# One ring of four PSUM banks in place of a bank for the keys and a ring of three

## The chip, the core and the metric

The kernel runs on one core of a Trainium2 chip. The metric is the device time of one execution in microseconds (us). The core's engines work from separate queues, each in its own order: TensorE (PE, with PEld for its weight loads), VectorE (DVE), ScalarE (ACT), GpSimd (POOL) and SyncE (SP), whose queue issues nearly all transfers here. Matmuls write to PSUM, which has eight banks, and ACT and DVE carry the results from there to SBUF.

## What is computed

Linear attention with a positive feature map, for 8 batches of 8 heads of 576 tokens, and then a mixer block on its output: mixing over the tokens, then over the channels.

```python
def phi(x):
    proj = np.einsum('bhsd,df->bhsf', x, w_phi)
    proj = proj - np.max(np.abs(proj), axis=-1, keepdims=True)
    return np.concatenate([np.exp(proj), np.exp(-proj)], axis=-1)
q_p, k_p = (phi(q), phi(k))
kv = np.einsum('bhsf,bhsd->bhfd', k_p, v)
z = np.sum(k_p, axis=2)
num = np.einsum('bhsf,bhfd->bhsd', q_p, kv)
den = np.einsum('bhsf,bhf->bhs', q_p, z)[..., None] + 1e-06
attention = num / den            # heads side by side become x: 8 x 576 x 512
xt = x.transpose(0, 2, 1)
h = np.maximum(xt @ w_tok1, 0.0) @ w_tok2
u = x + h.transpose(0, 2, 1)
h2 = np.maximum(u @ w_ch1, 0.0) @ w_ch2
out = u + h2
```

## The kernel before

Five streams are written as generators, and `weave` (L676) interleaves them in the program by the cost that each yields and a share given to it (L695). `keys()` (L283) goes over the 32 pairs of heads: it loads a pair (`raw`, `v`), splits it into a high and a low part (`stack`, tiles `stk`), projects five groups of tokens (`less_max`, L221, tiles `ppk`), and adds their exponentials `kp` into `pkv` (`add_kv`). `queries()` does the same for queries (`stq`, `ppq`, and the tail `ppt`), turns them, takes exponentials (`qf`, `qh`, `ql`) and multiplies them by the keys' sums (`numerators`, L504, tiles `pn`); the first eight pairs go another way (`pt`, `pr`, `pf`). `token_stream()` runs `token_mix` (L541) for each batch b in two halves h: transposes (`px`), a first product into `pa`, its relu (`ah` on ACT, `al` on DVE), and a second product into `ph`, which DVE adds to `xt` (L586). `channel_stream()` runs `channel_mix` (L590) on 18 blocks of 256 tokens, up (`h`, 24 matmuls for each of six tiles) and down (`acc`); a block starts when the batch it lies in is mixed. `load_weights()` brings in the weights. In a name such as `ph6_1_0_0` the first two numbers are the batch and the half; in `ppk30_1` and `pn28_01` the first is the pair of heads.

What is written so is not yet the order of the engines: from it a list scheduler makes each engine's queue, places the tiles, and adds the waits. It gives a tile a place when one of its pool is free, so that the number of banks in a pool decides which matmuls may come next.

The eight banks of PSUM: `ps_a` has two (`acc`, and the first batch's token mixing), `ps_h` one (`h`), `ps_k` one (`pkv`), and `ps_w` four. Three of these four form a ring, `REST` (L59), for queries, their turns, numerators, and token mixing from the second batch on (`bank`, L536). The fourth carries the tag "keys": the keys' projections (L236), every other projection of the first four pairs' queries (L233), and every other `h` of the last three blocks (L608). The keys' projections of the first four pairs are in `ps_a` (L227).

Of the kernel before, what the change touches and what calls it, by code (L numbers as in the profile page):

```python
# [8 lines left out]
F32 = mybir.dt.float32  # L9
# [8 lines left out]
P = 128  # L18
B, H, S, D = 8, 8, 576, 64
NP = H // 2  # L20
F = 128
# [16 lines left out]
CH = 256  # L38
# [9 lines left out]
def mixer_kernel(ctx, tc, qk, vm, vt, w_phi, w1, w2, wc1, wc2d, out):  # L48
# [5 lines left out]
    ps_w = ctx.enter_context(tc.tile_pool(name="ps_w", bufs=1, space=PSUM))  # L54
# [1 line left out]
    ps_h = ctx.enter_context(tc.tile_pool(name="ps_h", bufs=1, space=PSUM))  # L56
    ps_a = ctx.enter_context(tc.tile_pool(name="ps_a", bufs=1, space=PSUM))

    REST = dict(tag="rest", bufs=3)  # L59

    def streamed(pool, shape, dtype, **kw):

# [158 lines left out]
    def less_max(ts, units, name, base=None, early=False):  # L221

        n, kind = len(units), name[0]
        if early and base == D:
            ps = ps_a.tile([P, 2, 2, F], F32, tag=f"a{nplain['k'] % 2}", name=f"pp{name}")  # L227
            nplain["k"] += 1
        elif early and base == 0 and (nplain["q"] % 2 == 0 or nplain["q"] >= BORROWED):
            ps = ps_h.tile([P, 2, 2, F], F32, tag="h", name=f"pp{name}")  # L230
            nplain["q"] += 1
        elif early and base == 0:
            ps = ps_w.tile([P, 2, 2, F], F32, tag="keys", name=f"pp{name}", bufs=1)  # L233
            nplain["q"] += 1
        elif kind == "k":
            ps = ps_w.tile([P, 2, 2, F], F32, tag="keys", name=f"pp{name}", bufs=1)  # L236
        else:
            ps = ps_w.tile([P, 2, 2, F], F32, name=f"pp{name}", **REST)
        for i, u in enumerate(units):
            t, c = (ts[1], 512) if u is None else (ts[u[0]], P * u[1])  # L240
            if base is None:
                nc.tensor.matmul(ps[:, i].rearrange("p two f -> p (two f)"), t[:, c:c + P],  # L242
                                 wp2.rearrange("p two f -> p (two f)"), start=True, stop=True)
            else:
                rows = slice(D, P) if name == "k0_0" else slice(0, P)
                nc.tensor.matmul(ps[:, i, 0], t[rows, c:c + P], wz[rows, base // D], start=True, stop=True)  # L246
        if base is None:
            part = wk.tile([P, 2, F], F32, tag="part", name=f"part{name}")
            nc.scalar.copy(part[:, :n], ps[:, :n, 1])
            pr = wk.tile([P, 2, F], F32, tag="p", name=f"p{name}")  # L250
            nc.vector.tensor_tensor(pr[:, :n], ps[:, :n, 0], part[:, :n], op=ALU.add)
            pr, eng = pr[:, :n], nc.gpsimd
        else:
            pr, eng = ps[:, :n, 0], nc.vector
        mx = column(wk, 2, tag=f"mx{kind}", name=f"mx{name}")
        nc.vector.tensor_reduce(mx[:, :n], pr, axis=AX.X, op=ALU.max, apply_absolute_value=True)  # L256
        pm = wk.tile([P, 2, F], F32, tag=f"pm{kind}", name=f"pm{name}", bufs=1 if kind == "t" else 2)
        eng.tensor_tensor(pm[:, :n], pr, mx[:, :n].unsqueeze(2).to_broadcast([P, n, F]), op=ALU.subtract)  # L258
        return pm
# [160 lines left out]
    def turn(i, k, j, pm, tail, behind):  # L420
# [3 lines left out]
        else:  # L424
            ptr = ps_w.tile([P, 3, P], F32, **REST, name=f"pt{i}_{k}{j}")
            rows = [pm[:, 0], pm[:, 1]]
# [31 lines left out]
    def row_numerators(i, k, j, qps):  # L458
# [6 lines left out]
        if j == 0:  # L465
            sums[0] = ps_w.tile([P, 2, 3, D + 1], F32, **REST, name=f"pr{i}_{k}")
        pn = sums[0]
# [24 lines left out]
    def flip(i, k):  # L492
        b, p = divmod(i, NP)
        make_xts(b)
        x = rows_of[b, p // 2][k][:, :, (p % 2) * P:(p % 2) * P + P]
        pf = ps_w.tile([P, SEG[0][1]], F32, **REST, name=f"pf{i}_{k}")[:, :SEG[k][1]]
        for u in range(3 - k):
# [92 lines left out]
    def channel_mix(i, segs):  # L590
        uh, ul = [], []
        for c in range(NC_):
            h = streamed(wk, [P, CH], F32R, tag=f"uh{c}", name=f"uh{i}_{c}", bufs=1)
            l = streamed(wk, [P, CH], F32R, tag=f"ul{c}", name=f"ul{i}_{c}", bufs=1)
            d = 0
            for b, t, o, n, s in segs:
                nc.scalar.copy(h[:, d:d + n], t[:, c, o:o + n])  # L597
                nc.gpsimd.tensor_tensor(l[:, d:d + n], t[:, c, o:o + n], h[:, d:d + n].bitcast(F32),  # L598
                                        op=ALU.subtract)
                d += n  # L600
            uh.append(h)
            ul.append(l)
        yield 0
        acc = [ps_a.tile([P, 2, CH], F32, tag=f"a{k}", name=f"acc{i}_{k}") for k in range(2)]

        def up_proj(ep):
            if i >= LAST and ep % 2:
                ph = ps_w.tile([P, 2, CH], F32, tag="keys", name=f"h{i}_{ep}", bufs=1)  # L608
            else:
                ph = ps_h.tile([P, 2, CH], F32, tag="h", name=f"h{i}_{ep}")  # L610
            for k in range(2):
                es = slice((2 * ep + k) * P, (2 * ep + k + 1) * P)
                for c in range(NC_):
                    mm3(ph[:, k], (wc1_h[:, c, es], wc1_l[:, c, es]), (uh[c], ul[c]), c == 0, c == NC_ - 1)
            gh = streamed(wk, [P, 2, CH], F32R, tag="g", name=f"gh{i}_{ep}", bufs=4)
            gl = streamed(wk, [P, 2, CH], F32R, tag="g", name=f"gl{i}_{ep}", bufs=4)
            nc.scalar.activation(gh, ph, AF.Relu)  # L617
            nc.vector.scalar_tensor_tensor(gl, ph, 0.0, gh.bitcast(F32), op0=ALU.max, op1=ALU.subtract)  # L618
            return gh, gl

        def down_proj(ep, gh, gl):
            for a in range(2):
                for k in range(2):
                    e = 2 * ep + k
                    for c in (2 * a, 2 * a + 1):
                        cs = slice(c * P, (c + 1) * P)
                        mm3(acc[a][:, c % 2], (wc2[e][:, 0, cs], wc2[e][:, 1, cs]), (gh[:, k], gl[:, k]),
                            e == 0 and c % 2 == 0, e == NE - 1, group_ok=True)

        prev = None  # L630
        for ep in range(NE // 2):
            yield from until(lambda: 2 * ep + 1 in loaded)
            g = up_proj(ep)
            ups[0] += 1
            yield 2.6
            if prev is not None:
                yield from until(lambda: 2 * ep - 1 in loaded)
                down_proj(ep - 1, *prev)
                yield 2.6
            prev = g  # L640
        yield from until(lambda: NE - 1 in loaded)
        down_proj(NE // 2 - 1, *prev)
        yield 2.6
        for k in range(2):
            d = 0
            for b, t, o, n, s in segs:
                v = t[:, 2 * k:2 * k + 2, o:o + n]
                nc.vector.tensor_tensor(v, acc[k][:, :, d:d + n], v, op=ALU.add)
                nc.sync.dma_start(out[b, :, 2 * k:2 * k + 2, s:s + n], v)
                d += n  # L650
        yield 0
# [87 lines left out]
```

## Time and profile before

| What | Value |
|---|---|
| median of three runs | 1119.68 us (1118.68 to 1120.17) |
| the profiled execution, its own time | 1120.8 us |
| span of its trace | 1119.0 us |
| granted TensorE clock, mean | 0.995 |
| PE busy, share of the span | 98% |
| weight loads (PEld) | 96% |
| DVE, ACT, POOL | 63%, 50%, 51% |

An engine's busy share is of the whole span. Matmuls overlap in the records (one of 256 columns has a row of some 280 ns), so that PE reads busy while its matmuls follow more slowly than they could; the number of matmuls in a stretch (the x in brackets) tells more than the busy time. A wait is put down to the instruction that released it.

### The profile page before, as it was taken

The page shows a single profiled execution, that of the slowest core. Times are in us where ns is not written, and L with a number is a line of the kernel's source. Part 1 is how long each engine was busy: PE and PEld are TensorE (multiplying, and loading weights), DVE is VectorE, ACT ScalarE, POOL GpSimd, SP SyncE. Part 2 cuts the span into 40 slices and gives each one's busy share as a digit, 9 for nine tenths or more (in the row PEclk, how much of TensorE's full clock was granted, in tenths as well). Part 3 has the DMA queues.
Part 4 walks back from the last instruction along what each step waited for, and adds up shares of the span by engine and source line. Part 5 has one row for each costly group of instructions (what it writes and reads, how often), then busy time and mean ns, then how long its engine had stood idle before and what let it go on. Part 6 is the DMA issues. An engine that isn't in the chain of part 4 may idle for free.

```text
span 1119.0 us, 24637 instructions
## 1 busy us (share of the span) xinstructions
PE 1092.4 (98%) x9040; PEld 1073.2 (96%) x9040; DVE 708.9 (63%) x1775; ACT 556.1 (50%) x1589; POOL 567.0 (51%) x1047
## 2 busy tenths in 40 slices
PE   9999999999999999999999999999999989999998
PEld 8998999989998899999999999999999989999998
DVE  6889964467667676767666575764776776642111
ACT  4766553345546464656545464454565656441110
POOL 2334342367647665766656484663675766430110
PEclk9999999999999999999999999999999999999999
DMA  8545401133313232333323232122332232200000
GB/s 204 170 135 151 133 28 52 34 94 78 87 30 92 74 76 71 85 84 75 74 60 80 57 95 69 53 66 70 76 75 63 75 85 45 62 21 20 20 20 19
DMA packets 186744, 82.73 MB, mean 74 GB/s; under 512 B 159424, under 2 KB 171200, under 8 KB 186624
## 3 DMA queue, kind: packets, MB, share of 16 engines
q1 hardware_dynamic: 185104, 80.74, 27.9%
q8 instruction: 71, 1.16, 0.4%
q10 hardware_dynamic: 1520, 0.43, 0.2%
q14 instruction: 49, 0.40, 0.1%
HBM read 57.54 MB, written 23.59 MB: 73 GB/s over the span
## 4 chain that ended last, share of the span: by engine, by line
PE 77%; DVE 9%; POOL 4%; DMA 3%; ACT 3%; issue 2%; SPq 1%; ACTq 0%; POOLq 0%; DVEq 0%
PE h L87 24%; PE acc L87 23%; PE pkv L327 8%; PE pn L87 6%; PE ph L87 4%; PE pa L87 4%; PE pr L472 2%; PE ppk L242 2%; PE ppq L242 2%; DMA raw<-in_qk 1%; PE px L551 1%; DMA v<-in_vm 1%; PE ppq L246 1%; POOL pmq L258 1%; DMA qt<-dq 1%
## 5 line engine op out<-in xcount | busy, mean ns | idle before, releaser
L87 PE MATMUL acc<-gh,wc 128*128 128x256 f32 x1728 | 337.6, 282 | 0.0
L87 PEld LDWEIGHTS acc<-gh,wc 128*128 128x128 f32 x1728 | 273.6, 188 | 0.2
L87 PE MATMUL h<-uh,wc_h 128*128 128x256 f32 x864 | 244.1, 283 | 3.5 <-DVE gl L618 3.1
L87 PE MATMUL h<-uh,wc_l 128*128 128x256 f32 x864 | 244.1, 283 | 0.0
L87 PE MATMUL h<-ul,wc_h 128*128 128x256 f32 x864 | 242.9, 281 | 0.8 <-POOL ul L598 0.8
L87 PE MATMUL acc<-gl,wc 128*128 128x256 f32 x864 | 239.8, 281 | 0.0
L87 PEld LDWEIGHTS h<-uh,wc_h 128*128 128x128 f32 x864 | 162.5, 188 | 5.5 <-PE pn L87 2.8
L87 PEld LDWEIGHTS h<-ul,wc_h 128*128 128x128 f32 x864 | 162.7, 188 | 1.2 <-POOL ul L598 1.0
L87 PEld LDWEIGHTS acc<-gl,wc 128*128 128x128 f32 x864 | 162.5, 188 | 0.0
L87 PEld LDWEIGHTS h<-uh,wc_l 128*128 128x128 f32 x864 | 162.5, 188 | 0.0
L327 PE MATMUL pkv<-v,kp 128*128 128x65 f32 (+2 forms) x1152 | 160.2, 270 | 1.8 <-ACT kp L302 0.7
L327 PEld LDWEIGHTS pkv<-v,kp 128*128 128x128 f32 x1152 | 150.5, 192 | 3.5 <-ACT kp L302 1.6
L302 ACT ACTIVATE kp<-pmk 128x256 f32<-128x256 f32 (+1 forms) x320 | 108.5, 389 | 67.1 <-POOL pmk L258 43.9
L618 DVE SCALAR_TENSOR_TENSOR gl<-h,gh 128x512 fp32r<-128x512 f32 x108 | 73.5, 680 | 98.2 <-ACT gh L617 95.0
L447 POOL TENSOR_TENSOR ql<-qf,qh 128x320 fp32r<-128x320 f32 (+1 forms) x96 | 80.1, 834 | 72.4 <-ACT qh L446 72.1
L617 ACT ACTIVATE gh<-h 128x512 fp32r<-128x512 f32 x108 | 64.4, 596 | 101.1 <-PE h L87 99.4
L438 ACT ACTIVATE qf<-qt 128x320 f32<-128x320 f32 (+1 forms) x192 | 81.6, 437 | 63.0 <-POOL qf L437 29.0
L87 PE MATMUL pn<-qh,kv 128*128 128x320 f32 (+1 forms) x384 | 106.6, 308 | 3.8 <-ACT qh L446 1.6
L598 POOL TENSOR_TENSOR ul<-xt,uh 128x64 fp32r<-128x64 f32 (+3 forms) x120 | 60.6, 530 | 92.3 <-ACT uh L597 92.3
L446 ACT ACTIVATE qh<-qt 128x320 fp32r<-128x320 f32 (+1 forms) x192 | 82.9, 436 | 29.1 <-POOL qh L445 27.0
L217 POOL TENSOR_TENSOR stk<-raw,stk 64x512 fp32r<-64x512 f32 (+1 forms) x48 | 68.3, 1422 | 47.7 <-DVE stk L216 45.2
L258 POOL TENSOR_TENSOR pmk<-pk,mxk 128x256 f32<-128x256 f32 (+1 forms) x120 | 72.8, 606 | 36.0 <-DVE mxk L256 27.8
(129 smaller groups left out, 2293.1 us busy)
## 6 DMA issues: line engine op xcount, KB each, us to landing
raw<-in_qk SPq DMA_DIRECT2D x23, 576.0 KB, 4.2
rawc<-in_wc SPq DMA_DIRECT2D x24, 512.0 KB, 4.1
v<-in_vm SPq DMA_DIRECT2D x31, 256.0 KB, 4.1
dq<-tq SPq DMA_DIRECT2D x24, 320.0 KB, 2.1
qt<-dq SPq DMA_DIRECT2D x96, 80.0 KB, 2.9
dq<-tq SPq DMA_DIRECT2D x24, 256.0 KB, 2.0
qt<-dq SPq DMA_DIRECT2D x96, 64.0 KB, 2.9
out_x<-xt SPq DMA_DIRECT2D x12, 256.0 KB, 2.1
```

Source lines behind the costliest of these rows:

```text
L87: nc.tensor.matmul(o, a, m, start=first and i == 0, stop=last and i == 2, skip_group_check=group_ok)
L217: nc.gpsimd.tensor_tensor(t[lo:lo + D], src, t[base:base + D].bitcast(F32), op=ALU.subtract)
L242: nc.tensor.matmul(ps[:, i].rearrange("p two f -> p (two f)"), t[:, c:c + P], wp2.rearrange("p two f -> p (two f)"), start=True, stop=True)
L258: eng.tensor_tensor(pm[:, :n], pr, mx[:, :n].unsqueeze(2).to_broadcast([P, n, F]), op=ALU.subtract)
L302: nc.scalar.activation(kp[:, :len(us), sg], pm[:, :len(us)], AF.Exp, scale=1.0 - 2.0 * sg)
L327: nc.tensor.matmul(o, kp[:, n, sg], v, start=g == 0 and n == 0 and sg == 0, stop=u is None, skip_group_check=True)
L438: nc.scalar.activation(full, src, AF.Exp, scale=1.0 - 2.0 * sg)
L446: nc.scalar.activation(hi, src, AF.Exp, scale=1.0 - 2.0 * sg)
L447: (nc.gpsimd if sg else nc.vector).tensor_tensor(lo, full, hi.bitcast(F32), op=ALU.subtract)
L598: nc.gpsimd.tensor_tensor(l[:, d:d + n], t[:, c, o:o + n], h[:, d:d + n].bitcast(F32), op=ALU.subtract)
L617: nc.scalar.activation(gh, ph, AF.Relu)
L618: nc.vector.scalar_tensor_tensor(gl, ph, 0.0, gh.bitcast(F32), op0=ALU.max, op1=ALU.subtract)
```

## The change

The ring `REST` gets four banks in place of three, and the three uses of the tag "keys" become uses of the ring. The keys' projections therefore take whichever of the four banks comes free, as do all the others, and the others may take the bank that was the keys'. The number of banks in all stays at eight. No instruction is added or taken away: both programs have 8152 matmul instructions, with the same count for every tile's name and shape.

```diff
--- before.py
+++ after.py
@@ -56,7 +56,7 @@
     ps_h = ctx.enter_context(tc.tile_pool(name="ps_h", bufs=1, space=PSUM))
     ps_a = ctx.enter_context(tc.tile_pool(name="ps_a", bufs=1, space=PSUM))
 
-    REST = dict(tag="rest", bufs=3)
+    REST = dict(tag="rest", bufs=4)
 
     def streamed(pool, shape, dtype, **kw):
 
@@ -230,10 +230,10 @@
             ps = ps_h.tile([P, 2, 2, F], F32, tag="h", name=f"pp{name}")
             nplain["q"] += 1
         elif early and base == 0:
-            ps = ps_w.tile([P, 2, 2, F], F32, tag="keys", name=f"pp{name}", bufs=1)
+            ps = ps_w.tile([P, 2, 2, F], F32, name=f"pp{name}", **REST)
             nplain["q"] += 1
         elif kind == "k":
-            ps = ps_w.tile([P, 2, 2, F], F32, tag="keys", name=f"pp{name}", bufs=1)
+            ps = ps_w.tile([P, 2, 2, F], F32, name=f"pp{name}", **REST)
         else:
             ps = ps_w.tile([P, 2, 2, F], F32, name=f"pp{name}", **REST)
         for i, u in enumerate(units):
@@ -605,7 +605,7 @@
 
         def up_proj(ep):
             if i >= LAST and ep % 2:
-                ph = ps_w.tile([P, 2, CH], F32, tag="keys", name=f"h{i}_{ep}", bufs=1)
+                ph = ps_w.tile([P, 2, CH], F32, name=f"h{i}_{ep}", **REST)
             else:
                 ph = ps_h.tile([P, 2, CH], F32, tag="h", name=f"h{i}_{ep}")
             for k in range(2):
```

What it moves is the order that the scheduler makes. Three places follow; the rows are the instructions of one engine in their order.

First, PE at token mixing of batch 6, second half: the end of the first product, `pa6_1`, and the start of the second, `ph6_1`. Before:

```order
L87 MATMUL pa6_1_13908<-xh6_1_4_14078,w1_l_103 128x256
L327 MATMUL pkv29_13822<-v1_113,kp29_4_14098 128x2x65
L242 MATMUL ppk30_1_14255<-wp2_91,stk300_14130 128x256 x2
L87 MATMUL ph6_1_0_0_14109<-w2_h_104,ah6_1_14105 128x320
L87 MATMUL ph6_1_0_0_14109<-w2_l_105,ah6_1_14105 128x320
L87 MATMUL ph6_1_1_0_14117<-w2_h_104,ah6_1_14105 128x320
L87 MATMUL ph6_1_1_0_14117<-w2_l_105,ah6_1_14105 128x320
L242 MATMUL ppt29_14156<-wp2_91,stq291_14153 128x256
```

Now:

```order
L87 MATMUL pa6_1_13908<-xh6_1_4_14078,w1_l_103 128x256
L87 MATMUL ph6_1_0_0_14109<-w2_h_104,ah6_1_14105 128x320
L87 MATMUL ph6_1_0_0_14109<-w2_l_105,ah6_1_14105 128x320
L87 MATMUL ph6_1_1_0_14117<-w2_h_104,ah6_1_14105 128x320
L242 MATMUL ppk30_0_14136<-wp2_91,stk300_14130 128x256 x2
L87 MATMUL ph6_1_1_0_14117<-w2_l_105,ah6_1_14105 128x320
L327 MATMUL pkv29_13822<-v1_113,kp29_4_14098 128x2x65 x2
L242 MATMUL ppt29_14156<-wp2_91,stq291_14153 128x256
```

The key group `ppk30_1` and one matmul of `pkv29` stood between the last `pa6_1` and the first `ph6_1`; now nothing does. The group `ppk30_0`, which stood earlier still, is now among the `ph6_1`, and `ppk30_1` comes some 40 rows below. `pn28_01`, which stands ten rows below both pieces, took the bank that `ph6_1_0_0` had left; in the built program it now takes the one of `ppt29`.

Second, DVE at the same place, with the semaphores that each instruction waits for in brackets (DMAHW is a transfer). Before:

```order
L577 SCALAR_TENSOR_TENSOR al6_1_14106<-pa6_1_13908,ah6_1_14105 128x512 [waits Activation_49]
L251 TENSOR_TENSOR pt29_14160<-ppt29_14156,partt29_14158 128x128 [waits Activation_49,Pool_49]
L216 CAST stk310_14607<-raw31_14602 64x512 [waits DMAHW6_49]
L586 TENSOR_TENSOR xt0_6_11788<-ph6_1_0_0_14109,xt0_6_11788 128x320 [waits PE_49]
L256 TENSOR_REDUCE mxt29_14162<-pt29_14160 128x1 [waits DVE_49]
L586 TENSOR_TENSOR xt0_6_11788<-ph6_1_1_0_14117,xt0_6_11788 128x320 [waits PE_49]
L251 TENSOR_TENSOR pq29_00_14171<-ppq29_00_14166,partq29_00_14169 128x256 [waits Activation_49,Pool_49]
```

Now:

```order
L577 SCALAR_TENSOR_TENSOR al6_1_14106<-pa6_1_13908,ah6_1_14105 128x512 [waits Activation_49]
L251 TENSOR_TENSOR pk30_0_14141<-ppk30_0_14136,partk30_0_14139 128x256 [waits Activation_49]
L256 TENSOR_REDUCE mxk30_0_14143<-pk30_0_14141 128x2 [waits DVE_49]
L251 TENSOR_TENSOR pt29_14160<-ppt29_14156,partt29_14158 128x128 [waits Activation_49,Pool_49]
L586 TENSOR_TENSOR xt0_6_11788<-ph6_1_0_0_14109,xt0_6_11788 128x320 [waits PE_49]
L256 TENSOR_REDUCE mxt29_14162<-pt29_14160 128x1 [waits DVE_49]
L586 TENSOR_TENSOR xt0_6_11788<-ph6_1_1_0_14117,xt0_6_11788 128x320 [waits PE_49]
L251 TENSOR_TENSOR pq29_00_14171<-ppq29_00_14166,partq29_00_14169 128x256 [waits Activation_49,Pool_49]
```

The cast `stk310`, which waits for a transfer, stood ahead of the two adds of `ph6_1` to `xt`; now it stands 14 rows behind the first of them. The two steps of `ppk30_0` have come in ahead of `pt29`.

Third, PE at token mixing of batch 3, first half. Before:

```order
L87 MATMUL pa3_0_6152<-xl3_0_4_6366,w1_h_102 128x256
L87 MATMUL pa3_0_6152<-xh3_0_4_6365,w1_l_103 128x256
L87 MATMUL h5_0_6462<-uh5_3_6454,wc1_l_107 128x256
L87 MATMUL ph3_0_0_0_6420<-w2_h_104,ah3_0_6416 128x320
L87 MATMUL ph3_0_0_0_6420<-w2_l_105,ah3_0_6416 128x320
L87 MATMUL ph3_0_1_0_6491<-w2_h_104,ah3_0_6416 128x320
L87 MATMUL ph3_0_1_0_6491<-w2_l_105,ah3_0_6416 128x320
```

Now:

```order
L87 MATMUL h5_0_6462<-uh5_1_6442,wc1_l_107 128x256
L87 MATMUL h5_0_6462<-uh5_2_6448,wc1_h_106 128x256
L87 MATMUL h5_0_6462<-ul5_2_6449,wc1_h_106 128x256
L87 MATMUL h5_0_6462<-uh5_2_6448,wc1_l_107 128x256
L87 MATMUL h5_0_6462<-uh5_3_6454,wc1_h_106 128x256
L87 MATMUL h5_0_6462<-ul5_3_6455,wc1_h_106 128x256
L87 MATMUL h5_0_6462<-uh5_3_6454,wc1_l_107 128x256
L87 MATMUL ph3_0_0_0_6420<-w2_h_104,ah3_0_6416 128x320
L87 MATMUL ph3_0_0_0_6420<-w2_l_105,ah3_0_6416 128x320
L87 MATMUL ph3_0_1_0_6491<-w2_h_104,ah3_0_6416 128x320
L242 MATMUL ppk16_0_6510<-wp2_91,stk160_6504 128x256 x2
L87 MATMUL ph3_0_1_0_6491<-w2_l_105,ah3_0_6416 128x320
```

Between the last `pa3_0` and the first `ph3_0` stood one matmul. Now that last `pa3_0` stands 15 rows above the first row shown, and 22 matmul instructions of `h5_0` and `pkv15` are between.

## Rows read from the trace of the kernel before

**Rows 1.** The page: the span, and PE's busy time, share and instructions.

```profile
span 1119.0 us, 24637 instructions
...
PE 1092.4 (98%) x9040; PEld 1073.2 (96%) x9040; DVE 708.9 (63%) x1775; ACT 556.1 (50%) x1589; POOL 567.0 (51%) x1047
```

**Rows 2.** Stretches of 28 us: busy us (x instructions) of PE, PEld, DVE, ACT, POOL; PEclk, DMA share, GB/s.

```profile
0.00:28.00 28.00, 25.27 (x170) 22.46 (x171) 19.43 (x58) 13.59 (x36) 6.80 (x20) 1.00 0.81 204
224.00:252.00 28.00, 25.49 (x190) 24.25 (x189) 18.05 (x46) 13.81 (x42) 17.77 (x32) 0.94 0.37 91
336.00:364.00 28.00, 25.76 (x206) 24.31 (x205) 22.07 (x55) 17.77 (x56) 21.88 (x42) 1.00 0.36 88
364.00:392.00 28.00, 25.20 (x186) 23.98 (x186) 19.44 (x49) 13.92 (x42) 18.51 (x38) 0.94 0.30 74
476.00:504.00 28.00, 27.01 (x208) 26.16 (x207) 18.78 (x50) 15.67 (x50) 18.92 (x38) 0.94 0.35 82
896.00:924.00 28.00, 25.38 (x203) 24.42 (x203) 20.03 (x52) 15.29 (x45) 17.66 (x34) 1.00 0.33 85
1064.00:1092.00 28.00, 28.00 (x241) 28.00 (x240) 4.84 (x7) 4.29 (x9) 2.85 (x4) 1.00 0.06 20
1092.00:1120.00 28.00, 22.95 (x197) 22.74 (x195) 4.15 (x6) 2.39 (x4) 0.00 (x0) 0.99 0.06 19
```

**Rows 3.** Whom PE waited for: us in total, times, longest us.

```profile
PE h L87 <- DVE gl L618: 3.1, 5, 1.0
PE ph L87 <- ACT ah L576: 1.9, 4, 0.7
...
PE pn L87 <- DVE xt L586: 1.2, 1, 1.2
...
PE pn L87 <- DVE den L520: 0.7, 2, 0.4
PE ppk L242 <- DVE pk L251: 0.7, 2, 0.4
...
PE pa L87 <- DVE den L520: 0.4, 1, 0.4
PE px L551 <- DVE den L520: 0.4, 2, 0.2
...
PE ppq L242 <- DVE al L577: 0.2, 1, 0.2
```

**Rows 4.** Timeline, 900 to 911 us: start, us, engine, line, operation [idle before <-releaser].

```profile
902.78 0.42 DVE L216 CAST stk<-raw 64x512 fp32r<-64x512 f32 x1 [0.87 <-DMA raw<-in_qk]
903.23 0.49 DVE L586 TENSOR_TENSOR xt<-ph,xt 128x320 f32<-128x320 f32 x1
...
903.87 0.39 PE L87 MATMUL pn<-qh,kv 128*128 128x320 f32 x1 [1.25 <-DVE xt L586]
```

**Rows 5.** Groups by form: xcount | busy us, mean ns | idle before, releasers.

```profile
L251 DVE TENSOR_TENSOR pk<-ppk,partk 128x256 f32<-128x256 f32 x96 | 40.1, 418 | 20.5 <-ACT partk L249 13.0 <-POOL pmk L258 4.4 <-POOL pmq L258 2.0
...
L249 ACT COPY partk<-ppk 128x256 f32<-128x256 f32 x96 | 35.7, 372 | 25.6 <-PE ppk L242 23.2 <-DVE pq L251 1.3 <-DVE mxq L256 0.9
...
L586 DVE TENSOR_TENSOR xt<-ph,xt 128x320 f32<-128x320 f32 x32 | 15.5, 483 | 5.9 <-PE ph L87 5.7
...
L576 ACT ACTIVATE ah<-pa 128x512 fp32r<-128x512 f32 x16 | 9.6, 597 | 25.3 <-PE pa L87 25.3
```

**Rows 6.** Timeline of PE, 373 to 376 us.

```profile
373.03 0.42 PE L87 MATMUL ph<-w_h,ah 128*128 128x320 f32 x1 [0.69 <-ACT ah L576]
373.29 0.31 PE L87 MATMUL ph<-w_l,ah 128*128 128x320 f32 x1
373.44 0.31 PE L87 MATMUL ph<-w_h,ah 128*128 128x320 f32 x1
```

**Rows 7.** Timeline of PE, 436 to 438 us.

```profile
436.23 0.28 PE L87 MATMUL h<-uh,wc_l 128*128 128x256 f32 x1
437.08 0.41 PE L87 MATMUL ph<-w_h,ah 128*128 128x320 f32 x1 [0.57 <-ACT ah L576]
```

**Rows 8.** Whom DVE waited for, its waits for the raw keys and queries.

```profile
DVE stk L216 <- DMA raw<-in_qk: 15.7, 8, 4.0
```

## The prediction

> **What bounds the kernel now.** I read the page first: PE is busy for 98% of the span, and 26.6 us of 1119.0 are idle [rows 1]. So hardly anything can be won by shortening other engines; what can change is how closely the matmuls follow each other. Busy time hides some of that, so the table of stretches comes next, for the number of matmuls. In channel mixing alone, 28 us hold 241 matmuls of 256 columns, or 0.116 us each; that is the pace at which PE itself is the limit. Five stretches in the middle hold 186 to 208 [rows 2] (some of their matmuls have 320 columns and take 0.15 us [rows 6], which explains the smaller part of it). They are the times when a batch's token mixing runs, and a block of channel mixing can't start before it is done: PE then has only a chain (transposes, `pa`, relu, `ph`) and the attention's small pieces. Their idle time is 2.5 + 2.2 + 2.8 + 1.0 + 2.6 = 11.1 us. In three of them the granted clock is 0.94, that is 1.7 us of clock lost in each: the clock fell in stretches where PE had been short of work, and in none of the full ones. The start is idle for 2.7 us, and in the last row, of which 27 us lie within the span, for 4.0 us; 19.9 us lie between.
>
> Then whom PE waited for [rows 3]. The rows that name a reader of a bank of the ring, or of the keys' bank, are `pn` behind `xt` 1.2, `pn` behind `den` 0.7, `ppk` behind `pk` 0.7, `pa` and `px` behind `den` 0.4 each, and `ppq` behind `al` 0.2: 3.6 us. The others are for data, such as `h` behind `gl` 3.1 and `ph` behind `ah` 1.9, and the change frees none of those banks.
>
> **The change, part by part.** Instructions: none are added or removed, so the sum of the work stays. The bank of `h`, that of `pkv` and the two of `acc` are untouched. In the last three blocks every other `h` goes to the ring; nothing else is left there by then, the 24 matmuls of a down step cover its eviction, and the row of 241 matmuls shows PE full there already: no gain and no loss. The first batch's token mixing, in its own two banks, is not touched either.
>
> Bank turns. A turn is the distance on PE from the last matmul of one tile in a bank to the first of the next. A projection's bank needs a copy by ACT, 0.372, and an add by DVE, 0.418 [rows 5], and three handovers; one of them is the 0.15 us from the end of DVE's `xt` add at 903.72 to the matmul at 903.87 [rows 4], so the need is about 1.3 us. I counted the matmuls in each of the 584 turns of the four banks, in both built programs, at 0.117 us (256 columns) and 0.147 us (320 columns), an estimate from [rows 2, 6]. Before, 25 turns are shorter than 1.3 us and lack 9.2 us together; now 9 are, and lack 2.5 us. If the 3.6 us shrink alike, 1.0 is left: a gain of 2.6 us. Its ends are zero, if other waits fill the time, and 3.6.
>
> The clearest turn is the first place of the section on the change. Before, `pn28_01` took the bank of `ph6_1_0_0`, 0.8 us behind its last matmul, and PE stood for 1.25 us. DVE could not free the bank, since the cast `stk` stood in its queue, itself waiting 0.87 us for the keys' transfer [rows 4]. Now `pn28_01` takes the bank of `ppt29`, 1.4 us behind it, and the cast stands behind both adds. Both halves of that wait should go; it is the 1.2 us row. What comes next is `ph6_1_0_1`, which still needs the first add, six matmuls later.
>
> Cover that is lost. What may stand between the last `pa` and the first `ph` covers ACT's relu, 0.597 us [rows 5]. With nothing between, PE waited 0.69 us [rows 6]; with one matmul 0.57 [rows 7]. Batch 3's first half gains 22 matmul instructions there (the third place), so its 0.57 goes. Batch 6's second half loses a key group and one of `pkv`, 0.46 us, as the first place shows; batch 3's second half loses the same, and batch 1's goes from 0.70 us of matmuls to 0.29. That is 0.46 + 0.46 + 0.41 - 0.57, a cost of 0.8 us. It is the price of the ring: `ph` takes two of the four banks and the keys, who had their own, come later. The keys' sums are wanted only by later numerators, and add nothing themselves unless a pair's queries catch up with them.
>
> Net of these two: a gain of 1.8 us. The other bound takes every kind of short lead. With the same spacing of matmuls, the durations of the trace and 0.15 us a handover, I counted the places where a matmul's data or bank is ready less than 0.3 us ahead: 147 before, 107 now. The 19.9 us of idle time over 147 places is 0.135 us each, and 40 fewer make 5.4 us. The count leaves out how ACT, DVE and POOL queue, so it is an upper end. I take the middle of 1.8 and 5.4, 3.6 us. Moved transfers: SP's queue issues the same ones in another order, mostly in the first 100 us; the nearest row is DVE's wait for the keys and queries, 15.7 us in eight waits [rows 8], and I take no change for it, with both signs in the range.
>
> Here the Trainium skill would have it larger. Perfetto Trace Analysis, under "Identifying the Most-Contended Engine", says that a gap which repeats on the engine that should be full can mean that PSUM has no room for the next tile. The five short stretches are such a gap, and by that rule most of their 11.1 us would go; the rows of waits put only 3.6 us down to banks.
>
> The profiled execution took 1120.8 us; less 3.6 is 1117.2. The median lies 1.1 us below the profiled one, so it should come to 1116.1.
>
> **The rivals.** *The stretches fill up.* A free fourth bank lets token mixing and attention run further ahead, so that half of the 11.1 us goes, and one of the three falls of the clock: 5.6 + 1.7 = 7.3 us, 1112.4. All of the 11.1 us and all three falls would be 16 us, 1103.5, the outer end. For it speaks that the short stretches lie where the ring is in use; against it that most named waits are for data.
>
> *Nothing to be seen.* PE is the bound; a wait for a bank turns into one for the data of the same tile, since ACT, DVE and POOL carry as much as before. The named waits then trade places and the time stays at 1119.5. For it speaks that the order of the large pieces hardly moves: in both programs each batch's `pa` and `ph` stand within some 5 us of the same place on PE.
>
> *Slower: keys hold the ring.* With its own bank, a key group that is stuck in DVE's queue holds up only the next key group. In the ring it holds one of four banks, and PE, whose order is fixed, stands at the next tile that was given that bank. What sticks DVE is the cast that waits for a transfer: 15.7 us in eight waits, 2.0 on average and 4.0 at most [rows 8], against turns made for 1.3. If a third of that reaches PE it costs 5.2 us with no gain beside it: 1124.9. It outweighs the forecast's gain once more than 3.6 us, or about a quarter, get through. For it speaks the 0.8 us of cover already given away; against it the one case in the rows, where the cast has moved behind the adds. Another fall of the clock would add 1.7. TensorE: Matmul & The Clock Gate, "A second HAM failure mode: psum-queue depth-cycling", in the Trainium skill, says that cycling through PSUM's banks with short idle times lets the clock go down and up; no row here ties a fall to the number of banks.
>
> **How the numbers follow.** A measurement of this kernel can tell about 0.2%, 2.2 us, from no change: faster is below 1117.4, slower above 1121.9. The forecast, 1113 to 1119 around 1116, gets 0.38; the stretches that fill up 0.17; nothing to be seen 0.22; the held ring 0.23. Of the forecast's 0.38, 0.33 lie below 1117.4. Faster is then 0.50, the same 0.27, slower 0.23. The range from 1108 to 1125 leaves out the outer end of the second case (0.06) and the upper part of the last (0.10).
>
> **What would show it.** In the changed kernel's waits of PE, the row of `pn` behind `xt` should be gone, and those behind `den` and `pk` smaller; PE at the second half of batch 6 should not stand at `pn`, while `ph` behind `ah` should keep about 2 to 3 us. The short stretches should hold a few matmuls more, the full ones the same 241. The granted clock should fall three times, near the same places. I am wrong if PE's idle time grows at `pn`, `px` or `ppq` behind `pk` or `pq`, if DVE's waits for `raw` come up as waits of PE, or if a fourth fall appears.

## The result: 0.5 to 0.7% slower

| What | Before | Changed |
|---|---|---|
| median of three runs | 1119.68 us | 1128.20 us (1126.70 to 1129.68) |
| ratio, 95% interval | | 1.0073 [1.0058, 1.0087] |
| the same again, six runs | 1120.68 us | 1126.56 us, 1.0053 [1.0038, 1.0068] |
| span of the profiled execution | 1119.0 us | 1126.4 us |
| granted TensorE clock, mean | 0.995 | 0.992 |

The forecast was 1116 us, with a range from 1108 to 1125. The work is the same, as [rows 1] against the page of the changed kernel shows:

```profile
span 1126.4 us, 24762 instructions
...
PE 1095.5 (97%) x9040; PEld 1078.8 (96%) x9040; DVE 709.7 (63%) x1775; ACT 557.1 (49%) x1589; POOL 568.7 (50%) x1047
```

PE's idle time grew from 26.6 us to 1126.4 - 1095.5 = 30.9. The stretches that answer to [rows 2], and one more; columns: length, PE busy us (x matmuls), PEclk, DMA share, GB/s:

```profile
224.00:252.00 28.00, 26.69 (x219) 1.00 0.38 94
336.00:364.00 28.00, 26.52 (x207) 0.94 0.36 94
364.00:392.00 28.00, 25.68 (x211) 1.00 0.31 75
476.00:504.00 28.00, 26.48 (x214) 1.00 0.35 82
672.00:700.00 28.00, 26.58 (x208) 0.94 0.25 58
896.00:924.00 28.00, 24.47 (x169) 0.88 0.32 81
1064.00:1092.00 28.00, 28.00 (x241) 1.00 0.06 19
```

Four of the five short stretches did fill up a little, as the forecast had it (190 to 219, 206 to 207, 186 to 211, 208 to 214), in part because the falls of the clock have moved: three of the four had one before, one has one now. The fifth fell from 203 to 169, with two falls of the clock in it, and a stretch that had been nearly full, 672 to 700 (234 matmuls before), became a short one. The full stretch at the end has the same 241.

Whom PE waited for, against [rows 3]:

```profile
PE h L87 <- DVE gl L618: 5.2, 3, 2.0
PE pn L87 <- ACT qh L446: 3.6, 4, 1.3
PE ph L87 <- ACT ah L576: 2.8, 4, 0.7
PE pa L87 <- DVE xl L81: 1.6, 2, 0.8
...
PE acc L87 <- ACT gh L617: 1.2, 1, 1.2
...
PE ppk L242 <- DVE pk L251: 0.6, 1, 0.6
```

Of the 3.6 us put down to banks, 0.6 are left: the banks were set free as forecast. But `h` behind `gl` grew by 2.1 us, `ph` behind `ah` by 0.9, and `pn` behind `qh` is now the second row: waits for data took their place.

Where the wait at batch 6 went is seen around 903 to 917 us, the place of [rows 4]. DVE and PE, in order of time (start, us, operation, [idle before]):

```profile
902.64 0.38 PE L87 MATMUL pa<-xl,w_h 128*128 128x256 f32 x1 [0.80 <-DVE xl L81]
904.19 0.42 PE L87 MATMUL ph<-w_h,ah 128*128 128x320 f32 x1 [0.69 <-ACT ah L576]
...
913.41 0.87 DVE L216 CAST stk<-raw 64x512 fp32r<-64x512 f32 x1
...
915.04 0.92 DVE L216 CAST stq<-raw 64x512 fp32r<-64x512 f32 x1
...
916.31 0.64 DVE L618 SCALAR_TENSOR_TENSOR gl<-h,gh 128x512 fp32r<-128x512 f32 x1
...
917.10 0.36 PE L87 MATMUL h<-uh,wc_h 128*128 128x256 f32 x1 [2.02 <-DVE gl L618]
```

The cast `stk310`, which had moved behind the two adds, now stands with a cast of queries a few instructions ahead of `gl`, which frees the bank of the next `h`. The 1.25 us at `pn` are gone, and the wait at `h`, 1.0 us before, is 2.02. From 890 to 930 us PE is idle for 40 - 36.73 = 3.3 us before and for 40 - 36.47 = 3.5 now (the rows stand with e9 to e12): what was won at the bank was lost again within a few us.

### The profile page after: what moved, and what is told of

It reads as the page before. It is cut to its first block, busy times and chain, and to the rows that moved or that the text cites. A ratio compares the mean times of both kernels' runs of the same rounds, so it can differ in the third digit from the quotient of the medians.

```text
span 1126.4 us, 24762 instructions
## 1 busy us (share of the span) xinstructions
PE 1095.5 (97%) x9040; PEld 1078.8 (96%) x9040; DVE 709.7 (63%) x1775; ACT 557.1 (49%) x1589; POOL 568.7 (50%) x1047
## 4 chain that ended last, share of the span: by engine, by line
PE 79%; DVE 8%; DMA 4%; POOL 3%; ACT 2%; issue 2%; SPq 1%; ACTq 0%; POOLq 0%; DVEq 0%
PE h L87 24%; PE acc L87 23%; PE pkv L327 9%; PE pn L87 6%; PE ph L87 4%; PE pa L87 4%; PE pr L472 2%; PE ppk L242 2%; DMA qt<-dq 2%; PE ppq L242 2%; PE px L551 1%; PE ppk L246 1%; DMA pair<-in_qk 1%; PE ppq L246 1%; POOL stq L217 1%
## 5 line engine op out<-in xcount | busy, mean ns | idle before, releaser
L87 PE MATMUL h<-uh,wc_h 128*128 128x256 f32 x864 | 246.8, 286 | 5.4 <-DVE gl L618 5.2
L258 POOL TENSOR_TENSOR pmk<-pk,mxk 128x256 f32<-128x256 f32 (+1 forms) x120 | 69.9, 582 | 80.8 <-DVE mxk L256 77.1
L598 POOL TENSOR_TENSOR ul<-xt,uh 128x64 fp32r<-128x64 f32 (+3 forms) x120 | 63.5, 554 | 84.4 <-ACT uh L597 84.2
L446 ACT ACTIVATE qh<-qt 128x320 fp32r<-128x320 f32 (+1 forms) x192 | 83.3, 438 | 38.6 <-POOL qh L445 35.9
```

The lines of the kernel that those rows point to most:

```text
L87: nc.tensor.matmul(o, a, m, start=first and i == 0, stop=last and i == 2, skip_group_check=group_ok)
L446: nc.scalar.activation(hi, src, AF.Exp, scale=1.0 - 2.0 * sg)
```

## The experiments

Two measures are used throughout. **Excess** (in the expectations) is what each matmul's distance to the next exceeds the median of its kind, summed over a stretch of the trace. **Clock and rest** split a time: an execution's span times one minus its mean granted clock is the time that the half-speed stretches lost (half of their length), the remainder is all else; both are means over the runs of a kernel, as differences to the runs of the kernel before in the same comparison. Resampling the runs gives most of these differences an interval of 1 to 2 us either way (3 to 5 for the clock of e3 and e7); the clock of one run is known to 0.001, or 1.1 us. In the last columns are the profiled execution's matmuls in the first 112 us, and its granted clock in two stretches.

| Run | ratio [95%] | clock, us | rest, us | matmuls to 112 us | PEclk 0:120 | PEclk 890:930 |
|---|---|---|---|---|---|---|
| before | | | | 842 | 1.00 | 1.00 |
| e13 changed again | 1.0053 [1.0038, 1.0068] | +2.4 | +3.7 | 812 | 0.99 | 1.00 |
| e1 changed, `gl` urgent | 1.0052 [1.0033, 1.0070] | +2.7 | +2.5 | 817 | 0.99 | 0.96 |
| e2 before, `gl` urgent | 0.9993 [0.9983, 1.0003] | -0.2 | -0.3 | 848 | 1.00 | 1.00 |
| e3 changed, lag 0.03 | 1.0072 [1.0048, 1.0096] | +4.7 | +3.3 | 780 | 0.96 | 0.96 |
| e4 before, lag 0.03 | 0.9989 [0.9975, 1.0003] | -0.2 | -1.3 | 850 | 1.00 | 1.00 |
| e5 changed, raw on POOL | 1.0053 [1.0036, 1.0070] | +0.5 | +4.9 | 798 | 0.99 | 1.00 |
| e6 before, raw on POOL | 0.9984 [0.9973, 0.9995] | +0.5 | -2.3 | 844 | 1.00 | 1.00 |
| e7 before, `px` in the keys' bank | 1.0208 [1.0183, 1.0234] | +8.6 | +14.3 | 850 | 1.00 | 1.00 |
| e8 before, bank for keys only | 1.0058 [1.0037, 1.0079] | +1.1 | +5.0 | 795 | 0.99 | 1.00 |
| e9 held to the end | 1.0008 [0.9997, 1.0020] | +0.4 | +0.8 | 849 | 1.00 | 1.00 |
| e10 held to pair 6 | 1.0016 [1.0000, 1.0032] | +1.4 | +0.2 | 846 | 1.00 | 0.91 |
| e11 held from pair 7 | 1.0026 [1.0015, 1.0037] | -0.9 | +4.0 | 800 | 0.97 | 1.00 |
| e12 held but for 7 to 19 | 0.9999 [0.9988, 1.0010] | -0.1 | -0.4 | 848 | 1.00 | 1.00 |
| e14 held in 7 to 19 only | 1.0031 [1.0020, 1.0043] | +1.0 | +2.5 | 806 | 0.99 | 0.96 |
| e15 held from pair 20 | 1.0010 [0.9998, 1.0023] | -0.4 | +1.8 | 809 | 0.99 | 1.00 |
| e16 held for early queries | 1.0050 [1.0036, 1.0064] | +3.1 | +2.7 | 812 | 0.99 | 0.91 |
| e17 as e12, raw on POOL | 0.9975 [0.9960, 0.9990] | -0.2 | -2.6 | 842 | 1.00 | 1.00 |
| e18 as e6, `gl` urgent | 0.9985 [0.9976, 0.9994] | -0.5 | -1.4 | 841 | 1.00 | 1.00 |

The excess up to 112 us, in which the expectations speak, divides the profiles in the same way as the column of matmuls: it is 13.9 to 15.8 us in the ten with the start as before, and 18.1 to 22.0 in the nine with the start shared and in e8 (all by the medians of the kernel before).

### Is it the luck of an order? e1 to e4

Two edits that rearrange the queues were made in both kernels: `gl` at high priority, and another lag of the interleaving.

```diff
-            nc.vector.scalar_tensor_tensor(gl, ph, 0.0, gh.bitcast(F32), op0=ALU.max, op1=ALU.subtract)
+            with tc.high_priority():
+                nc.vector.scalar_tensor_tensor(gl, ph, 0.0, gh.bitcast(F32), op0=ALU.max, op1=ALU.subtract)
```

```diff
-LAG = 0.02
+LAG = 0.03
```

> The ring of four, with one edit: DVE's step gl (L618), which frees the bank of h, is given priority over what else stands ready on DVE. PE's order stays the same but for a few rows. Theory Q (queues: the ring put the casts stk and stq directly ahead of gl, and raw loads ahead of the qt transfers): PE's wait of h for gl, 5.2 us, falls under 2 us, one or two of the five falls of the clock go, and the time comes to 1122 to 1125. Theory K (keys lose by sharing, whatever the queues): the wait goes to the next tile, 1126 to 1129. Theory L (luck of the order, the ring itself costs nothing): anything from 1118 to 1130.

> The kernel before with the same edit, as the control of it. Its wait of h for gl is 3.1 us. Theory Q: that falls to under 1.5 us, 1117 to 1119.5, a smaller gain than on the ring. Theory K: the same gain as on the ring. Theory L: within 3 us of before either way.

> The ring of four with one number of the weave moved (LAG 0.02 to 0.03), which reorders some instructions on every engine and has nothing to do with banks. Theory K: the loss stays, 1125 to 1130. Theory L: the time moves by several us, down to 1119 or up to 1133. Theory Q: between, 1123 to 1130, since the casts and loads stay where the ring puts them.

> The kernel before with the same number moved (LAG 0.02 to 0.03). Theory L: it loses as much as the ring did, 1123 to 1130, since the order before was a lucky one. Theories K and Q: within 3 us of before, 1117 to 1123.

With the changed kernel both edits leave 0.5 to 0.7% of loss; the kernel before stays within 0.1% of itself. So the loss goes with the change and does not hang on one lucky order, as far as two reorderings can show it. As a test of `gl` behind the casts e1 failed: PE's row of `h` behind `gl` kept its 5.2 us in three waits, since the priority did not bring `gl` ahead of them.

### Is it the late transfers? e5 and e6

In the changed kernel SP stands longer at a raw load (L269) whose buffer isn't free, with the turned queries (`qt`) queued behind it. The waits of ACT, SP and DVE in the changed kernel (us, times, longest):

```profile
ACT qf L438 <- DMA qt<-dq: 41.2, 21, 3.6
```

```profile
SPq L269 <- POOL stk L217: 39.4, 10, 7.3
```

```profile
DVE stk L216 <- DMA raw<-in_qk: 1.2, 2, 0.8
```

Before, the first was 19.6 us in 11 waits, the second 9.7 in 6; DVE's wait was the 15.7 us of [rows 8]. The edit takes the raw loads off SP's queue:

```diff
-        nc.sync.dma_start(raw[lo:hi], qk[i, lo:hi])
+        nc.gpsimd.dma_start(raw[lo:hi], qk[i, lo:hi])
```

> The changed kernel, with the transfers of raw (L269) issued from GpSimd's queue in place of SP's. In the changed kernel SP's queue stood 39.4 us in ten waits at a raw transfer for its buffer, with the transfers of the turned queries (qt) behind it, and ACT waited 41.2 us for qt in place of 19.6. Theory Q (queues: the late qt makes the loss): the waits for qt fall back to about 20 us or less, and at least half of the 8.5 us goes, a ratio of at most 1.004 to the kernel before. Theory K (keys lose by sharing a bank, whatever the queues): the waits for qt fall, the ratio stays at 1.005 to 1.009, and the first 112 us keep about 4 us more of excess matmul spacing than the kernel before.

> The same edit in the kernel before, as a control: raw is issued from GpSimd's queue. Both theories: within 0.3% of the kernel before. If it gains as much as the changed kernel does from the same edit, the late qt is no part of what the ring costs.

The waits for `qt` fell only to 35.9 us, and the changed kernel stayed at 1.0053. The kernel before gained from the same edit (0.9984), so what the edit gives is no part of what the ring costs. A later run speaks against it more plainly: e12 lost nothing, with as much waiting for `qt` as the changed kernel:

```profile
ACT qf L455 <- DMA qt<-dq: 42.0, 19, 4.4
```

### Which sharing? e7 and e8

One half of the change at a time, in the kernel before: another tile borrows the keys' bank (e7), or the others leave it (e8).

```diff
-                px = bank(b, [P, 2, P], f"px{b}_{h}_{u}", 1)
+                px = bank(b, [P, 2, P], f"px{b}_{h}_{u}", 1) if b == 0 else ps_w.tile([P, 2, P], F32, tag="keys", name=f"px{b}_{h}_{u}", bufs=1)
```

```diff
-            ps = ps_w.tile([P, 2, 2, F], F32, tag="keys", name=f"pp{name}", bufs=1)
+            ps = ps_w.tile([P, 2, 2, F], F32, name=f"pp{name}", **REST)
...
-                ph = ps_w.tile([P, 2, CH], F32, tag="keys", name=f"h{i}_{ep}", bufs=1)
+                ph = ps_w.tile([P, 2, CH], F32, name=f"h{i}_{ep}", **REST)
```

> The kernel before, with the transposes of token mixing (px, batches 1 to 7) put in the keys' bank, so that the ring of three is relieved of them and the keys share their bank with one kind of tile only. Half of the change: others borrow the keys' bank, and the keys borrow none. Theory K: the keys' bank is now held by px for one short turn at a time, and keys are hardly later: ratio 0.998 to 1.002. Theory S (sharing itself costs, any sharing of the keys' bank with token mixing): 1.003 or more, and a fourth fall of the clock.

> The kernel before, with the opposite edit: the keys' bank is for keys alone; the early queries that lay in it and the h of the last three blocks go to the ring of three. If what costs in the changed kernel is that keys of the first pairs meet queries in one ring, this one should keep the first 112 us at 14 us of excess or less (before: 14.3, changed: 18.1); if it is only that the early queries left the keys' bank and go through the ring, it shows the 18 as well. The last blocks have nothing else in the ring, so they should not change. Time: theory K 0.998 to 1.002; theory that the early queries' move makes the first loss, 1.003 to 1.005.

e7 lost 2.1%, more than either theory said: one fixed bank for both is worse than a ring, and says little of it (with the keys behind it, the granted clock is 0.83 and 0.87 in the two stretches from 336 to 392 us). e8 was the surprise. It touches only the early queries and the last blocks' `h`, and lost 0.58%, with 795 matmuls in the first 112 us against 842. From 168 us on its matmuls keep pace, so that with a ring of three the start suffers from the early queries' place alone, somewhat more than the second theory said.

### Where in time? e9 to e12

A form that gives the bank back in parts: the ring has four banks, and a tile `own` takes one of them, once, and holds it for the pairs that `own(i)` names; what had the keys' bank before is written into it. `own` is always true in e9, `i < 7` in e10, `i >= 7` in e11; in e12 it is

```diff
+    def own(i):
+        return i < 7 or i >= 20
+
+    def keys_bank(i, shape, name):
+        if not own(i):
+            return ps_w.tile(shape, F32, name=name, **REST)
+        if not own(i - 1) and i not in held or not held:
+            held[i] = ps_w.tile([P, 512], F32, name=f"own{i}", **REST)
...
-            ps = ps_w.tile([P, 2, 2, F], F32, name=f"pp{name}", **REST)
+            ps = keys_bank(int(name[1:].split("_")[0]), [P, 2, 2, F], f"pp{name}")
```

> A control for the next three. The ring has four banks as in the changed kernel, but one of them is taken once, by a tile own0, and held to the end; all that had the keys' bank in the kernel before is written into it. So it is the kernel before in another form. Every theory: ratio 0.998 to 1.002, the excess of matmul spacing in the first 112 us about 14 us (before 14.3, changed 18.1).

> The keys' bank is held for the early queries and the keys of pairs 4 to 6 (to about 150 us), and then given up: from pair 7 on all four banks are a ring, as in the changed kernel. Theory E (the loss starts early: keys and queries of the first pairs meet in the ring; block 1 starts 4.1 us later in the changed kernel): the first 112 us are as before at 14 to 15 us, and half of the loss goes, ratio 1.002 to 1.005. Theory T (the loss is in the later batches, where block 7 still stands at +0.3 us and blocks 14 to 17 at +7): ratio 1.006 to 1.008.

> The counterpart: a ring of four banks in the first 150 us, from pair 7 on a bank of the keys' own again (held by one tile to the end). Theory E: the first 112 us show 17 us of excess or more, and about 4 us of the loss stay, ratio 1.003 to 1.005. Theory T: 0.998 to 1.002, whatever the first 112 us show.

> The keys' bank is held to pair 6 and again from pair 20 on; in between the four banks are a ring. In the changed kernel block 1 starts 4.1 us later than before and block 7 only 0.3 us later, so that the ring seems to win 3.8 us between 170 and 560 us. Theory M (the ring is worth something in the middle, and costs at the ends): ratio 0.995 to 0.998. Theory N (it costs or does nothing everywhere, and the block times only show another order): 0.999 to 1.004.

The control e9 is the kernel before within its interval. e10 and e11 split the loss in two of different kinds. Sharing in the first 150 us (e11) costs 4.0 us of rest, 3.2 to 4.9 by resampling, and no clock; sharing from pair 7 on (e10) costs clock, 1.4 us (0.1 to 2.7), and hardly any rest. Sharing in the middle alone (e12) costs nothing in the whole. The first 112 us (of the first two also the first 168), and 890 to 930 us, of the kernel before, of the changed one, of e10 and of e11 in this order:

```profile
0.00:112.00 112.00, 106.23 (x842) 1.00 0.59 165
0.00:168.00 168.00, 162.16 (x1323) 1.00 0.48 137
890.00:930.00 40.00, 36.73 (x296) 1.00 0.30 74
```

```profile
0.00:112.00 112.00, 103.18 (x811) 1.00 0.57 162
0.00:168.00 168.00, 159.18 (x1281) 0.99 0.48 137
890.00:930.00 40.00, 36.47 (x273) 0.91 0.26 66
```

```profile
0.00:112.00 112.00, 105.57 (x846) 1.00 0.59 167
890.00:930.00 40.00, 36.47 (x272) 0.91 0.32 76
```

```profile
0.00:112.00 112.00, 101.70 (x800) 0.98 0.57 161
890.00:930.00 40.00, 36.88 (x295) 1.00 0.28 74
```

e10 has the start of the kernel before and the end of the changed one, e11 the reverse. Theory M of e12, a gain of 0.2 to 0.5% in the middle, is not borne out as time. But the middle is not even. Two stretches of the kernel before, and of e12:

```profile
168.00:400.00 232.00, 223.15 (x1813) 0.99 0.27 68
400.00:700.00 300.00, 297.01 (x2480) 0.99 0.30 75
```

```profile
168.00:400.00 232.00, 224.88 (x1850) 0.99 0.28 70
400.00:700.00 300.00, 293.77 (x2433) 0.99 0.30 72
```

To 400 us e12 gains 37 matmuls, some 13 of them because the clock fell once there and not twice; by 700 us it has lost 47. The changed kernel has 1861 and 2433, so it makes up for its late start by block 7 and then falls behind once more. This is no accident of one trace: the excess from 400 to 700 us is 19.3 to 23.3 us in the ten profiles with sharing there, and 15.0 to 17.0 in the nine others (without e7). What loses the gain again was not isolated.

### Do the parts add up? e13 to e16

e13 is the changed kernel again; e14 to e16 use the same form with `own(i)` as `7 <= i < 20`, `i >= 20` and `i < 4`.

> The changed kernel once more, beside the partial forms. If the parts add up to it, 1.004 to 1.005 here too and the 1.0073 was high; if they need each other, 1.006 to 1.009 again.

> A ring of four in the first 150 us and from pair 20 on, the keys' bank held from pair 7 to 19 between. Theory A (the parts add up): 0.26% for the start and about 0.16% for the end, ratio 1.003 to 1.005. Theory I (the start's delay makes the end worse): 1.006 to 1.009, with the two falls of the clock at 900 to 920 us.

> A ring of four up to pair 19 (about 585 us), then a bank of the keys' own and of the last h. Theory A: the start's 0.26% alone, ratio 1.001 to 1.004, no fall at 900 to 920 us. Theory J (the start's delay makes the middle worse): 1.005 or more.

> The bank is held only for what the early queries (pairs 0 to 3) had there, and given up behind them; keys of pairs 4 to 31 go through the ring of four. Against the run in which it was held to pair 6 (1.0016): if the early queries' place makes the loss of the start, the first 112 us stay at 16 us of excess or less and the ratio at 1.001 to 1.003; if it is the keys of pairs 4 to 6, the excess is 17 us or more and the ratio 1.004 to 1.008.

As ratios they do, within the intervals: e10 and e11 together make 0.42%, e14 with both ends shared 0.31%, the changed kernel again 0.53%. Between these and the first comparison's 0.73% what is left is 0.2%, about the width of an interval. Sharing at the end costs little where the start was held (e10 against e12, 0.17%) and 0.43% where it was not (e13 against e15); that the two need each other is not shown, since e14 lies only 0.05% above e11.

With the early queries' bank held but the keys of pairs 4 to 6 in the ring (e16), the loss is 0.50%; with these three pairs held too (e10) it is 0.16%, and the rest goes from +2.7 to +0.2 us. So these keys alone are enough for a loss. They are not all of it. Matmuls in the first 64 us, of the kernel before, of the changed one, and of e16 (there also the first 112):

```profile
0.00:64.00 64.00, 60.91 (x476) 1.00 0.68 184
```

```profile
0.00:64.00 64.00, 59.40 (x459) 1.00 0.66 177
```

```profile
0.00:64.00 64.00, 61.00 (x478) 1.00 0.70 184
0.00:112.00 112.00, 104.25 (x812) 0.98 0.60 164
```

By 64 us the changed kernel is 17 matmuls behind, 17 x 0.117 = 2.0 us, and e16 none. The keys of pair 4 have hardly begun by then: DVE has taken the maxima of 21 groups of keys before and of 20 now, five for each pair, and those of the first four pairs lie in `ps_a` in both kernels. What is late is queries, and already in the first 32 us (DVE's group of their maxima over these, before and now; columns as in [rows 5]):

```profile
L256 DVE TENSOR_REDUCE mxq<-ppq 128x2 f32<-128x256 f32 x7 | 2.8, 413 | 0.5 <-PE ppq L246 0.5
```

```profile
L256 DVE TENSOR_REDUCE mxq<-ppq 128x2 f32<-128x256 f32 x5 | 2.0, 413 | 0.5 <-PE ppq L246 0.5
```

So the first loss is that of the early queries, to which e16 gives their bank back, and it comes while DVE is not full (23.4 of 32 us in both kernels). The second begins with the keys of pair 4, and there DVE is full, with the splitting of the weights in the same queue. A stretch of all engines (busy us of PE, PEld, DVE, ACT, POOL) and DVE's group of the keys' maxima over the first 112 us, first of the kernel before, then of the changed one:

```profile
84.00:112.00 28.00, 25.50 (x205) 23.71 (x204) 27.07 (x65) 17.39 (x43) 13.26 (x14) 1.00 0.52 151
```

```profile
L256 DVE TENSOR_REDUCE mxk<-ppk 128x2 f32<-128x256 f32 (+1 forms) x32 | 12.3, 388 | 4.4 <-PE ppk L246 4.2
```

```profile
84.00:112.00 28.00, 24.80 (x196) 22.92 (x196) 27.88 (x64) 16.74 (x41) 14.80 (x15) 1.00 0.48 148
```

```profile
L256 DVE TENSOR_REDUCE mxk<-ppk 128x2 f32<-128x256 f32 (+1 forms) x29 | 11.3, 394 | 3.7 <-PE ppk L246 3.5
```

DVE is busy for 27.07 and 27.88 of the 28 us, and three groups of keys are late by 112 us. PE is 842 - 811 = 31 matmuls short there, 31 x 0.117 = 3.6 us, and by 168 us 1323 - 1281 = 42, with a fall of the clock between. Until the first `h`, which starts at 77.0 us before and at 80.4 now, PE has only keys, queries and the first batch's token mixing, so that what comes late has nothing beside it. The two losses do not simply add: e16 is without the first, and yet has 812 matmuls by 112 us, as the changed kernel has, with a fall of the clock at 107 us. Which turn of which bank begins either was not isolated, and no run shares a ring of four with the early queries alone.

### Does the middle hold a gain? e17 and e18

> The form with the keys' bank held to pair 6 and from pair 20 on (a ring of four between; 0.9999), with raw (L269) issued from GpSimd's queue. If the late qt hid a gain of the ring in the middle, ACT's waits for qt fall below 30 us and the ratio is 0.996 or less, better than the same edit gave the kernel before (0.9984). If sharing gives nothing there, 0.997 to 1.000.

> The kernel before with both edits that it took without loss: raw issued from GpSimd's queue (0.9984) and gl at high priority (0.9993). If they add, 0.9977, which would be faster than both kernels; if the first alone counts, 0.998 to 0.999; if they get in each other's way, 1.000 or more.

e17, with a ring in pairs 7 to 19 alone and the raw loads on GpSimd's queue, is faster than both kernels: 1116.48 us, 0.9975 [0.9960, 0.9990]. Whether the ring has a part in it is open: the raw loads alone gave 0.9984 [0.9973, 0.9995] in another comparison, and the waits for `qt` stayed at 36.2 us, so no hidden gain behind them was shown. The edits of e18 do not add (0.9985).

## Why the prediction was wrong, step by step

**Work unchanged, full stretches unchanged**: right (9040 matmul records, 241 in the full stretch).

**Bank turns, a gain of 2.6 us**: the waits went as said, 3.6 to 0.6 us with `pn` behind `xt` and behind `den` gone. As time it was not there. e12, which shares in the middle alone, lies at -0.4 us of rest against +0.8 in its control, with overlapping intervals, and its ratio to the kernel before leaves a gain of 1.3 us at most; e10, in which the 1.2 us of `pn` behind `xt` are gone too (e12 still has 1.1), lies at +0.2. What the ring gave up to 400 us it lost by 700. The upper bound of 5.4 us, from counting short leads, was no bound on anything that PE felt. The Trainium skill's rule that stands beside it (Perfetto Trace Analysis, "Optimization Strategy", the section behind the one that the prediction names: repeating gaps can mean too little room in PSUM) would have had more; the trace doesn't agree, since four of the gaps filled by 1 to 29 matmuls, in part because a fall of the clock had gone from them, and the time did not follow.

**Cast and `pn28_01`**: half right. That wait went; but the cast came to stand ahead of `gl`, and the wait of `h` grew from 1.0 to 2.0 us. It does so in every one of e1, e3, e10, e13, e14 and e16 (1.6 in e5), where pairs from 20 on share, and stays at 1.0 in e9, e11, e12 and e15. I followed the cast past the adds and not to the next instruction behind it.

**Lost cover, 0.8 us**: right in the sum, `ph` behind `ah` grew by 0.9, and at batch 6, from 0.22 to 0.69. In part this is luck: the waits that are new in the second halves of batches 1 and 3 are 0.70 and 0.69 us against 0.41 and 0.46 in the sum, and a wait of 0.40 at batch 7, which the sum leaves out, went.

**The step that failed**: what the start loses was put at nothing. "The keys' sums are wanted only by later numerators, and add nothing themselves unless a pair's queries catch up with them" is one half of it; the early queries, which the change moves into the ring, have no term at all, and what is moved in the first 100 us got "no change". What was put at zero is the largest term: 2.5 to 4.9 us of rest in e1, e3, e5, e11, e13, e14 and e16, and 1.8 in e15, all with the start shared; -1.3 to +0.8 in e2, e4, e9, e10 and e12, with the start as before and raw loads where they were. In the first batches nothing else is there for PE, so that late queries (17 matmuls behind by 64 us) and late keys (31 in all by 112 us) are late matmuls. I looked at that stretch as one row of 2.7 idle us and at its transfers, not at which groups would come later, nor at DVE, which is full from 84 to 112 us.

**The clock, three falls**: wrong, and this is the second term. By the mean clock, the half-speed stretches lost 3.3 us in 107 runs of the kernel before, 6.0 in e13 and 8.6 in the first comparison. Three of the five in the profiled execution, and one stretch at full speed behind them:

```profile
112.60:116.00 3.40, 3.40 (x18) 0.50 0.79 252
904.50:907.90 3.40, 3.40 (x16) 0.50 0.71 206
918.10:921.50 3.40, 3.40 (x18) 0.51 0.24 96
921.50:924.90 3.40, 3.40 (x30) 0.99 0.63 101
```

A fall is 3.4 us at 1.2 GHz, 16 to 18 matmuls in place of 30, or about 1.7 us. The three of the kernel before lay at other places; the changed one has five. I had a fourth as the sign of being wrong, and priced it at 1.7 us, but had no row from which to see it come.

**The rivals**: "nothing to be seen" described the waits best (bank waits became data waits). "Keys hold the ring" came nearest in time, 1124.9, by another mechanism: DVE did not stick at the raw transfers, whose waits fell to 1.2 us, and the keys did not block the ring but came late in it. The eight forms with a shared start lost 3.2 us of rest on average, the seven of these comparisons with a shared end 2.3 us of clock (0.5 to 4.7): 5.5 us, against 5.9 measured in e13, which is itself in both means. The first comparison's 8.5 us had 8.6 - 3.3 = 5.3 us of clock in it if its own runs of the kernel before lost as much as the 107; the one of them whose clock is on record lost 5.6, which leaves 3.0. Why the clock fell oftener there than in e13, the same kernel, stays open.

## What to carry to other kernels

A bank that looks like a luxury may be what paces the start: look at a pool change first in the stretch where TensorE has little else to do and the next stage waits for the whole of a batch, and count there which groups will come later, of every kind of tile that changes its place; an engine that is full (here DVE, 27 of 28 us) is a second place to look, and not the first. Waits that the profile puts down to a bank can all go without any time, when the next instruction's data was as late; to see a part of a pool change alone, hold one place of the ring by a tile for the pairs in question. And follow a moved instruction to all that stands behind it at its new place, not only to what it has left.

## What was not expected of the hardware

The falls of the clock came with the place of sharing more regularly than with any single wait. All nine profiles in which the ring is shared in the start, and e8, have one before 120 us; none of the ten others has. In the mean over the runs this early fall is no added cost: e11 and e15 lose 0.9 and 0.4 us less to the clock than the kernel before. Of the eight in which pairs from 20 on share, six have one or two at 890 to 930 us; none of the other twelve. But it is not decided by the waits: e13 has the same 0.8, 0.7 and 2.0 us of waits there as the first profile of the same kernel, and a granted clock of 1.00 throughout that stretch, where the first had 0.91. The Trainium skill (TensorE: Matmul & The Clock Gate, "A second HAM failure mode: psum-queue depth-cycling") tells of a clock that goes down and up when work cycles through PSUM's banks with short idle times between. The runs agree in part. The seven comparisons in which pairs from 20 on share the larger ring lose 0.5 to 4.7 us more to the clock, but e11, e12 and e15, with the larger ring elsewhere, lose no more than the kernel before, and e7, whose ring is no larger, loses 8.6 more. Whether the cycling itself is the cause or the waits for data beside it, no run here tells apart; of the 34 matmuls fewer in the stretch from 896 to 924 us, the two falls themselves make 26 (16 and 18 in place of 30 each).
